# Choosing the FFN units of an agent-attention MoE kernel by two searched limits instead of by a rank over all keys

## The chip, the cores and the metric

The kernel runs on one core of one Trainium2 chip. The metric is device time of the whole launch in microseconds (us), the median of three runs.

## The reference

There are four batches of N = 11456 tokens with 128 channels, and 49 agents per batch. Attention goes from agents to keys and back from queries to agents; its output is the input x of a mixture of eight experts with F = 1024 hidden units, of which each token uses the best one.

```
a2k = softmax(agents @ k.T / sqrt(128));  agent_v = a2k @ v
x   = softmax(q @ agents.T / sqrt(128)) @ agent_v
expert = argmax(normalize(x) @ normalize(expert_emb).T / tau)
out = gate * (relu(x @ w1[expert]) @ w2[expert])
```

So x of a token is a positive mixture of the 49 rows of agent_v, and what it gives at a hidden unit is the same mixture of the 49 values of agent_v @ w1 at that unit.

## The kernel before

For each batch the kernel forms agent_v (`av_chain`), takes the expert that most tokens of the batch will use, loads its w1 and w2 (`load_expert`) and multiplies agent_v by w1 (`gp`, kept in `gts`): 49 values g for each of the 1024 units. A unit whose 49 values have one sign is linear for every token: relu does nothing or gives zero. So the units are sorted by the key (sum g)^2 / (sum g^2), which is 49 where all values are equal and small where signs are mixed:

- the 256 units with the smallest keys (FM = 2 x 128) go through a real relu: their weights are gathered into `gh` and `gl` (high and low halves in 16 bits) and `w2p`;
- all others are taken as linear, and of these the positive ones are summed into one matrix `lin`;
- the next 320 units (FV) are gathered into `vm`, and `proved` tests for every token that their sign is the expected one; the rest is covered by a bound (`far`) on the token's weights. Tokens that fail (strays) are found in `mark_strays` and computed singly by `fix`, or by a loop at the very end.

All of this is `pick_expert`, a generator that is run beside the rest. A unit sits at (partition p, column c) with c from 0 to 7. The rank of a unit was found so: the key is cut to its upper bits and the unit number is written into the lower ones, so that no two are equal (L773 to L777); matmuls with the identity copy all 1024 keys to every partition (`row`, L796, evicted by ScalarE at L798); four passes on VectorE count the smaller keys for columns 0 to 3 (L810) and four on ScalarE sum signs for columns 4 to 7 (L812, corrected at L819). From the rank come one-hot matrices `sel` (L822 for the 256, L899 for the 320), and matmuls with these gather: `placed` (L831) the weights agent_v @ w1, `w2pp` (L871) the rows of w2. L852 makes `lin`.

The whole program is unrolled; a planner sets the order of the instructions on each engine, and every engine then works through its own queue in that order. In batch 0 nothing else is to be done while units are chosen, so there `in_place` fixes an instruction's place behind a named one, and zero matmuls (`zero_products`, ZV, ZG, ZB of them) fill TensorE's queue. In batches 1 to 3 the choice runs beside the FFN of the batch before: `ffn_mm1` (L1222, L1223), evictions `hh` on ScalarE (L1226) and `hl` on VectorE (L1227), `ffn_mm2` (L1250 to L1252), `proved` (L1093 to L1099), and the keys and queries of other batches (L418 to L436). A `yield g` lets the other generators place their work before the next lines.

Of the kernel before, what the change touches and what calls it, by code (L numbers as in the profile page):

```python
# [18 lines left out]
P = 128  # L19
# [10 lines left out]
def kernel(ctx: ExitStack, tc: tile.TileContext, q, k, v, agents, emb, tau, w1, w2, out):  # L30
# [9 lines left out]
    FW = 4 * P  # L40
# [28 lines left out]
    ZV, ZG, ZB = 3, 2, 6  # L69
# [235 lines left out]
    uid = cst.tile([P, NF], I32, name="uid")  # L305
# [22 lines left out]
    def setup():  # L328
# [8 lines left out]
        with in_place(i_):  # L337
            pool.iota(iotaf, pattern=[[1, FW]], base=0, channel_multiplier=0, allow_small_or_imprecise_dtypes=True)
            pool.iota(uid, pattern=[[P, NF]], base=0, channel_multiplier=1)
            pool.iota(iota8m, pattern=[[1, E]], base=64, channel_multiplier=0, allow_small_or_imprecise_dtypes=True)  # L340
            pool.iota(pidx, pattern=[[0, 1]], base=0, channel_multiplier=1, allow_small_or_imprecise_dtypes=True)
        dve.tensor_tensor(out=fold, in0=ident[:, :A], in1=ident[:, LO : LO + A], op=ALU.add)
        with in_place(i_):
# [6 lines left out]
            pool.memset(cnt_p, 0.0)  # L350

    def setup2():

        dve.tensor_scalar(tri, iotaf[:, :P], pidx, None, ALU.is_gt)
# [27 lines left out]
    a_last, f_last, n_last, c_last, v_last = [], [], [], [], []  # L382
# [291 lines left out]
    def pick_expert(b, g):  # L674
# [36 lines left out]
        flat = sel.rearrange("p c f -> p (c f)").bitcast(F32)  # L711
        row = flat[:, F:]
        junk = [sel.rearrange("p c f -> p (c f)")[:, i * F : (i + 1) * F] for i in range(2)]
# [8 lines left out]
        act.activation(junk[0], w1s, AF.Square, accum_out=sq[0])  # L722
# [21 lines left out]
        def second():  # L744
# [14 lines left out]
        mean, key, nkey, sgn, pw = col("mean"), col("key"), col("nkey"), col("sgn"), col("pw")  # L759
        gsq = flat[:, : NF * A].rearrange("p (c a) -> p c a", a=A)  # L760
# [3 lines left out]
        ki = key.bitcast(I32)  # L764
# [43 lines left out]
        rank, more = col("rank"), col("more")  # L808
# [27 lines left out]
        dve.scalar_tensor_tensor(out=mask, in0=rank, scalar=FM - 0.5, in1=pos, op0=ALU.is_ge, op1=ALU.mult)  # L836
# [5 lines left out]
        for h in (1, 0):  # L842
            e_last = vec.tensor_tensor(out=gts[:, :, h, :A], in0=ga, in1=mask.unsqueeze(2).broadcast_to([P, NF, A]), op=ALU.mult)
# [884 lines left out]
```

## Time and profile before

| | |
|---|---|
| median of 3 runs | 704.52 us (702.52 to 705.45) |
| the profiled execution | 704.34 us |
| its span in the profile | 702.5 us |
| TensorE (PE) busy | 646.8 us, 92% of the span |
| VectorE (DVE) busy | 542.2 us, 77% |
| ScalarE (ACT) busy | 488.0 us, 69% |
| GpSimd (POOL) busy | 341.7 us, 49% |

The span is the time from the first to the last instruction of the core; the rest of the device time lies around it. Busy is the sum of an engine's instruction times, and matmuls overlap each other. Times in the timelines count from the span's start. Batch 0 chooses its units between 67 and 87 us, batches 1 to 3 around 217 to 259, 385 to 430 and 545 to 595 us.

### The profile page before, as it was taken

To read this page: it belongs to the slowest core of one execution; us is meant where nothing else is said; L and a number is where in the kernel's file an instruction comes from. 1 tells how busy PE (TensorE), PEld (TensorE's weight loads), DVE (VectorE), ACT (ScalarE), POOL (GpSimd) and SP (SyncE) were. 2 spreads that over 40 slices of the span, in tenths; PEclk is the share of its full clock that TensorE was granted. 3 is DMA by queue.
4 is the path that set the end of the run, shared out by engine and by line. 5 is a ranking of instruction groups with operands and counts; after the bars stand their busy time and mean duration, and the time that the engine had idled before them with its cause. 6 is when DMAs were issued, how large, how long until landed. Compare 5 with 4: busy or idle time off the path is not lost. (4 is left out here: it accounts for less than half of the span.)

```text
span 702.5 us, 23300 instructions
## 1 busy us (share of the span) xinstructions
PE 646.8 (92%) x9168; PEld 531.3 (76%) x9168; DVE 542.2 (77%) x1485; ACT 488.0 (69%) x1350; POOL 341.7 (49%) x578
## 2 busy tenths in 40 slices
PE   8998897999999899899999789899999979998995
PEld 6886786777788587688887568688888768786685
DVE  4755996875669998756777999896576898977993
ACT  3555687797778856687778856868668863878841
POOL 6000247384415836656524553567463563976400
PEclk9998999999999899999999999999999999999999
DMA  8986099959778359949796539949576526233121
GB/s 342 291 277 250 2 242 256 215 154 264 177 238 246 87 141 260 215 149 230 242 239 168 119 84 243 243 127 249 138 182 201 134 74 151 62 92 110 61 79 70
DMA packets 163136, 124.73 MB, mean 178 GB/s; under 512 B 82874, under 2 KB 139280, under 8 KB 163026
## 3 DMA queue, kind: packets, MB, share of 16 engines
q1 hardware_dynamic: 149586, 99.54, 55.3%
q10 hardware_dynamic: 13120, 23.47, 9.8%
q8 instruction: 73, 1.20, 0.7%
q14 instruction: 37, 0.30, 0.1%
q0 software_dynamic: 320, 0.23, 0.1%
HBM read 80.26 MB, written 23.79 MB: 148 GB/s over the span
## 5 line engine op out<-in xcount | busy, mean ns | idle before, releaser
L1227 DVE SCALAR_TENSOR_TENSOR hl<-hp,hh 128x512 f16<-128x512 f32 (+1 forms) x184 | 122.5, 668 | 33.0 <-ACT hh L1226 32.4
L1250 PE MATMUL yp<-w2p,hh 128*128 128x128 f16 x720 | 139.2, 221 | 3.9 <-ACT hh L1226 3.9
L1251 PE MATMUL yp<-w2p,hh 128*128 128x128 f16 x720 | 139.0, 220 | 0.0
L1252 PE MATMUL yp<-w2p,hl 128*128 128x128 f16 x720 | 136.1, 221 | 0.3 <-DVE hl L1227 0.3
L1097 ACT ACTIVATE under<-vp 128x320 f16<-128x320 f32 (+1 forms) x268 | 118.5, 442 | 24.8 <-PE vp L1093 20.1
L1226 ACT ACTIVATE hh<-hp 128x512 f16<-128x512 f32 (+1 forms) x184 | 107.4, 590 | 39.6 <-PE hp L1223 28.3
L1093 PE MATMUL vp<-vm,tt 128*128 128x320 f16 x360 | 96.6, 302 | 7.6 <-ACT under L1097 3.0
L425 ACT COPY fT<-fTp 128x512 f32<-128x512 f32 (+1 forms) x136 | 75.5, 573 | 29.1 <-PE fTp L418 20.6
L436 PEld LDWEIGHTS sp<-aT_all,fT 128*64 128x64 f32 x2336 | 79.9, 138 | 17.9 <-issue 8.4
L436 PE MATMUL sp<-aT_all,fT 128*64 128x49 f32 x2336 | 92.5, 225 | 1.0 <-DVE aT_all L206 0.4
L1250 PEld LDWEIGHTS <-hh 128*128 128x128 f16 x720 | 72.0, 100 | 20.0 <-ACT hh L1226 7.4
L1252 PEld LDWEIGHTS <-hl 128*128 128x128 f16 x720 | 71.5, 99 | 15.4 <-issue 4.7
L1251 PEld LDWEIGHTS <-hh 128*128 128x128 f16 x720 | 71.6, 100 | 5.8 <-issue 0.6
L960 POOL TENSOR_TENSOR e<-qe,e 128x392 f16<-128x392 f32 (+1 forms) x46 | 42.7, 927 | 64.5 <-ACT e L959 62.5
L1222 PE MATMUL hp<-tt,gh 128*128 128x512 f16 (+1 forms) x184 | 69.2, 377 | 4.6 <-DVE vmin L1099 3.6
L1265 DVE TENSOR_TENSOR ot<-yp,gs 128x512 f32<-128x512 f32 (+1 forms) x92 | 61.4, 670 | 11.0 <-PE yp L1252 8.7
L1223 PE MATMUL hp<-tt,gl 128*128 128x512 f16 (+1 forms) x184 | 69.3, 377 | 0.0
L1044 POOL TENSOR_TENSOR nrm<-qq,half 128x16 f32<-128x16 f32 (+2 forms) x28 | 68.9, 2461 | 0.2
L1241 PE MATMUL yp<-lin,tt 128*128 128x128 f16 x720 | 62.0, 220 | 1.2 <-DVE ot L1265 1.2
L1005 POOL TENSOR_TENSOR rt<-rt 128x384 f32<-128x384 f32 (+1 forms) x48 | 40.3, 840 | 43.9 <-DVE rt L1002 42.2
L418 PE MATMUL fTp<-ident,qt 128*128 128x128 f32 (+1 forms) x344 | 55.0, 288 | 5.3 <-ACT under L1097 2.2
L1099 DVE TENSOR_REDUCE vmin<-vp 128x1 f32<-128x320 f32 (+1 forms) x92 | 44.1, 480 | 17.2 <-PE vp L1093 16.8
(359 smaller groups left out, 1575.5 us busy)
## 6 DMA issues: line engine op xcount, KB each, us to landing
kt<-in_k_dram SPq DMA_DIRECT2D x44, 512.0 KB, 7.4
vt<-in_v_dram SPq DMA_DIRECT2D x44, 512.0 KB, 6.5
out_dram<-ot ACTq DMA_DIRECT2D x88, 256.0 KB, 3.1
qt<-in_q_dram SPq DMA_DIRECT2D x42, 512.0 KB, 6.1
w1s<-in_moe_w_dram SPq DMA_DIRECT2D x9, 512.0 KB, 4.3
w2s<-in_moe_w_dram SPq DMA_DIRECT2D x9, 512.0 KB, 6.7
q<-in_q_dram SPq DMA_DIRECT2D x2, 512.0 KB, 11.3
tt<-e SPq DMA_TRANSPOSE x46, 3.9
```

What stands on the lines that cost most here:

```text
L425: act.copy(dst, tp[:, : m * p])
L436: i = pe.matmul(out=s[h : h + w, c * A : (c + 1) * A], lhsT=xT[:, c * p + h : c * p + h + w], rhs=rhs, start=True, stop=True, skip_group_c ...
L1044: pool.tensor_tensor(out=nrm, in0=quad, in1=half[:, :n], op=ALU.pow)
L1093: pe.matmul(out=z[:p, :FV], lhsT=tts[b, u][:, c * p : (c + 1) * p], rhs=bt.vm, start=True, stop=True)
L1097: act.activation(under[:p], z[:p, :FV], AF.Relu, scale=-1.0, accum_out=bt.vsum[:p, at])
L1222: pe.matmul(out=hp[:, :m], lhsT=bt.gh[:, fs], rhs=tt, start=True, stop=False)
L1223: pe.matmul(out=hp[:, :m], lhsT=bt.gl[:, fs], rhs=tt, start=False, stop=True)
L1226: h_last[:] = [act.activation(hh[:, :m], hp[:, :m], AF.Relu)]
L1227: dve.scalar_tensor_tensor(out=hl[:, :m], in0=hp[:, :m], scalar=0.0, in1=hh[:, :m], op0=ALU.max, op1=ALU.subtract)
L1250: pe.matmul(out=y, lhsT=hh[:, cs], rhs=wh, start=False, stop=False, skip_group_check=True)
L1251: pe.matmul(out=y, lhsT=hh[:, cs], rhs=wl, start=False, stop=False, skip_group_check=True)
L1252: y_last[:] = [pe.matmul(out=y, lhsT=hl[:, cs], rhs=wh, start=False, stop=last, skip_group_check=True)]
```

## The change

The rank is replaced by two limits. The key is scaled so that it lies between 0 and 4096. First VectorE compares each of a partition's 8 keys with 64 limits 0, 1, 4, ..., 63^2, and eight matmuls of a column of ones with the result add up over units: every partition gets, for each limit, how many of the 1024 keys are below it. The number of limits with at most 256 (and at most 576) keys below gives the step in which the limit lies. The same is done again with 32 finer limits for each of the two (the wanted counts come in as one more matmul), and the largest finer limit with no more than the wanted count is taken. A unit is a member of the 256, or of the 320, if its key is below its limit; its place is the number of members before it, from matmuls with a triangle (same column) and with ones (columns before). Places that stay empty in the 320 are masked in `vm` by adding 1024 to the test value. The bound `far` comes from the second limit.

In batch 0 the low half of w2 (`w2x[:, :, 1]`) moves from before the rank to after the one-hot writes, the scores of the next batch's units 2 and 3 move behind the first count and behind the placing, and the zero matmuls are divided differently (ZB from 6 to 1, and 2, 4 and 3 before the new groups). The constants `iotaf` start at 1 instead of 0, and `sel` and `vm` get 320 columns instead of 512.

```diff
+    T1, T2 = 64, 32
+    KQ = T1 * T1 / A
...
-    ZV, ZG, ZB = 3, 2, 6
+    ZV, ZG, ZB, ZC = 3, 2, 1, (2, 4, 3)
+    HOP = 2
...
-                act.activation(w2x[:, :, 0], w2s, AF.Copy, scale=s3)
-                with in_place(n_last):
-                    dve.scalar_tensor_tensor(out=w2x[:, :, 1], in0=w2s, scalar=s3, in1=w2x[:, :, 0], op0=ALU.mult, op1=ALU.subtract)
+                s_last[:] = [act.activation(w2x[:, :, 0], w2s, AF.Copy, scale=s3)]
...
-        dve.tensor_tensor(out=key, in0=key, in1=pw, op=ALU.mult)
-        yield 1
-        dve.tensor_scalar(ki, ki, 0x7FFFFC00, None, ALU.bitwise_and)
-        yield 1
-        dve.tensor_scalar(key, key, 2.0 ** -100, None, ALU.max)
-        yield 1
-        dve.tensor_tensor(out=ki, in0=ki, in1=uid, op=ALU.bitwise_or)
-        yield 1
-        n_ = dve.tensor_scalar(nkey, key, -1.0, None, ALU.mult)
...
+        dve.scalar_tensor_tensor(out=key, in0=key, scalar=KQ, in1=pw, op0=ALU.mult, op1=ALU.mult)
+        yield 1
+        def count(i, thrs):
+            n_ = dve.tensor_tensor(out=below[i], in0=key.unsqueeze(2).broadcast_to([P, NF, T1]),
+                                   in1=thrs.unsqueeze(1).broadcast_to([P, NF, T1]), op=ALU.is_lt)
+            if b == 0:
+                n_last[:] = [n_]
+            yield HOP * g
+            t_ = psx("count")
+            if b == 0:
+                zero_products(t_, ZC[i], z_last if i else c_last)
+            t_ = t_[:, :T1]
+            for c in range(NF):
+                i_ = pe.matmul(out=t_, lhsT=one16.broadcast_to([P, P]), rhs=below[i][:, c], start=(c == 0), stop=(c == NF - 1 and i == 0))
+            if i:
+                i_ = pe.matmul(out=t_, lhsT=one16.broadcast_to([P, P]), rhs=caps.rearrange("p k t -> p (k t)"), start=False, stop=True)
+            if b == 0:
+                g_last[:] = [i_]
+                if i == 0:
+                    z_last[:] = ahead_s(2, g_last, pss)
+            yield g
+            return t_
+        t_ = yield from count(0, firsts)
...
+        at, top2 = sm.tile([P, 2], F32, name="at", tag="at"), sm.tile([P, 2], F32, name="top2", tag="top2")
+        for k_, cap in enumerate((FM, FM + FV)):
+            dve.tensor_scalar(below[1][:, k_], t_, cap + 0.5, 0.0, ALU.is_lt, ALU.add, accum_out=at[:, k_ : k_ + 1])
+        yield 1
+        fine = sm.tile([P, 2, T2], F32, name="fine", tag="fine")
+        dve.tensor_tensor(out=fine, in0=steps, in1=at.unsqueeze(2).broadcast_to([P, 2, T2]), op=ALU.add)
+        yield 1
+        dve.tensor_tensor(out=fine, in0=fine, in1=fine, op=ALU.mult)
+        yield 1
+        s3, i3 = yield from second()
+        fine_ = fine.rearrange("p k t -> p (k t)")
+        t_ = yield from count(1, fine_)
...
-        s3, i3 = yield from second()
+        dve.scalar_tensor_tensor(out=fine_, in0=t_, scalar=0.5, in1=fine_, op0=ALU.is_lt, op1=ALU.mult)
+        yield 1
+        dve.tensor_reduce(out=top2, in_=fine, axis=AX.X, op=ALU.max)
+        yield 1
+        dve.tensor_scalar(member[:, 0, :NF], key, top2[:, :1], None, ALU.is_lt)
+        yield 1
+        dve.scalar_tensor_tensor(out=member[:, 1, :NF], in0=key, scalar=top2[:, 1:], in1=member[:, 0, :NF], op0=ALU.is_lt, op1=ALU.subtract)
+        yield HOP * g
+        t_ = psx("place")
+        if b == 0:
+            zero_products(t_, ZC[2], g_last)
+        t_ = t_[:, : 2 * (NF + 1)]
+        pv = t_.rearrange("p (k c) -> p k c", k=2)
+        for c in range(NF + 1):
+            i = pe.matmul(out=pv[:, :, c:], lhsT=one16.broadcast_to([P, P]) if c else tri, rhs=member[:, :, : NF + 1 - c],
+                          start=(c == 0), stop=(c == NF), skip_group_check=True)
+        if b == 0:
+            l_last[:] = [i]
+            z_last[:] = ahead_s(3, l_last, psh)
+            for u in range(2, NEXT):
+                ahead_copy(u, s_last)
...
-        for h in range(2):
-            t_ = psx("row")
-            hs = slice(h * 512, h * 512 + 512)
-            for c in range(NF // 2):
-                i = pe.matmul(out=t_[:, c * P : (c + 1) * P], lhsT=key[:, h * NF // 2 + c : h * NF // 2 + c + 1].broadcast_to([P, P]),
-                          rhs=ident, start=True, stop=True)
-            act.copy(row[:, hs], t_)
-            if b == 0 and h:
-                g_last[:] = [i]
-                z_last[:] = g_last
-                for u in range(2, NEXT):
-                    z_last[:] = ahead_s(u, g_last, psh if u == 3 else pss)
-            yield g
...
-        for c in range(NF // 2):
-            dve.tensor_scalar(junk[0], row, key[:, c : c + 1], 0.0, ALU.is_lt, ALU.add, accum_out=rank[:, c : c + 1])
-            d = c + NF // 2
-            i = act.activation(junk[1], row, AF.Sign, bias=nkey[:, d : d + 1], accum_out=more[:, d : d + 1])
-            if b == 0:
-                s_last[:] = [i]
-            yield g
-        for u in range(2, NEXT) if b == 0 else ():
-            ahead_copy(u, s_last)
-        hi = slice(NF // 2, NF)
-        dve.tensor_scalar(rank[:, hi], more[:, hi], -0.5, (F - 1) / 2, ALU.mult, ALU.add)
+        rank = sm.tile([P, 2, NF], F32, name="rank", tag="rank")
+        dve.scalar_tensor_tensor(out=rank, in0=pv[:, :, :NF], scalar=1.0, in1=member[:, :, :NF], op0=ALU.add, op1=ALU.mult)
+        if b > 0:
+            dve.tensor_scalar(vm, iotaf[:, :FV], pv[:, 1, NF:], 1024.0, ALU.is_gt, ALU.mult)
...
-            dve.tensor_scalar(sel[:, c, :FM], iotaf[:, :FM], rank[:, c : c + 1], None, ALU.is_equal)
+            n_ = dve.tensor_scalar(sel[:, c, :FM], iotaf[:, :FM], rank[:, 0, c : c + 1], None, ALU.is_equal)
...
+        if b == 0:
+            n_last[:] = [n_]
+        if b == 0:
+            with in_place([n_]):
+                dve.tensor_scalar(vm, iotaf[:, :FV], pv[:, 1, NF:], 1024.0, ALU.is_gt, ALU.mult)
+            with in_place(n_last):
+                dve.scalar_tensor_tensor(out=w2x[:, :, 1], in0=w2s, scalar=s3, in1=w2x[:, :, 0], op0=ALU.mult, op1=ALU.subtract)
...
-        dve.scalar_tensor_tensor(out=mask, in0=rank, scalar=FM - 0.5, in1=pos, op0=ALU.is_ge, op1=ALU.mult)
+        dve.scalar_tensor_tensor(out=mask, in0=key, scalar=top2[:, :1], in1=pos, op0=ALU.is_ge, op1=ALU.mult)
...
-            e_last = vec.tensor_tensor(out=gts[:, :, h, :A], in0=ga, in1=mask.unsqueeze(2).broadcast_to([P, NF, A]), op=ALU.mult)
+            with in_place(n_last if b == 0 else ()):
+                e_last = vec.tensor_tensor(out=gts[:, :, h, :A], in0=ga, in1=mask.unsqueeze(2).broadcast_to([P, NF, A]), op=ALU.mult)
...
-        dve.tensor_scalar(mask, rank, FM + FV - 0.5, BIG, ALU.is_lt, ALU.mult)
-        dve.tensor_scalar(rank, rank, -float(FM), None, ALU.add)
-        yield 1
-        dve.tensor_tensor(out=mask, in0=mask, in1=key, op=ALU.add)
-        yield 1
-        dve.tensor_reduce(out=gmx[:, 1:], in_=mask, axis=AX.X, op=ALU.min)
...
+        dve.tensor_scalar(bt.far, top2[:, 1:], -1.0 / KQ, A + 0.1, ALU.mult, ALU.add)
...
-                dve.tensor_scalar(sel[:, c, :FV], iotaf[:, :FV], rank[:, c : c + 1], sgn[:, c : c + 1], ALU.is_equal, ALU.mult)
+                dve.tensor_scalar(sel[:, c, :FV], iotaf[:, :FV], rank[:, 1, c : c + 1], sgn[:, c : c + 1], ALU.is_equal, ALU.mult)
...
-        dve.tensor_scalar(vm, placed(0, FV), thr, None, ALU.subtract)
+        dve.scalar_tensor_tensor(out=vm, in0=placed(0, FV), scalar=thr, in1=vm, op0=ALU.subtract, op1=ALU.add)
```

## Rows read from the trace of the kernel before

**Rows 1.** Timeline of VectorE, batch 0: start us, length us, line, operation.

```profile
69.28 0.17 DVE L771 TENSOR_TENSOR key<-key,pw 128x8 f32<-128x8 f32 x1
...
70.37 0.17 DVE L777 TENSOR_TENSOR key<-key,uid 128x8 int32<-128x8 int32 x1
...
72.13 1.27 DVE L751 SCALAR_TENSOR_TENSOR w1s<-w2s,hsc,w1s 128x1024 f16<-128x1024 f32 x1
...
73.36 1.28 DVE L810 TENSOR_SCALAR_CACHE_REDUCE sel<-sel,key 128x1024 f16<-128x1024 f32 x1
...
77.33 1.28 DVE L810 TENSOR_SCALAR_CACHE_REDUCE sel<-sel,key 128x1024 f16<-128x1024 f32 x1
...
78.61 1.66 DVE L822 TENSOR_SCALAR sel<-iotaf,rank 128x256 f16<-128x256 f16 x8
...
82.54 0.41 DVE L839 CAST gl<-placed 128x256 f16<-128x256 f32 x1
```

**Rows 2.** Timeline of TensorE, batch 0; in brackets idle time and its releaser.

```profile
70.69 2.02 PE L796 MATMUL row<-ident,key 128*128 128x128 f32 x16 [1.47 <-DVE hiv L255]
...
72.64 2.07 PE L436 MATMUL sp<-aT_all,fT 128*64 128x49 f32 x64
...
74.64 1.47 PE L190 MATMUL placed<-zeros 128*128 128x512 f16 x6
...
82.88 1.92 PE L871 MATMUL w2pp<-w1s,sel 128*128 128x256 f16 x16
...
86.97 0.38 PE L1222 MATMUL hp<-tt,gh 128*128 128x512 f16 x1
```

**Rows 3.** Windows: length, busy us (x instructions) PE, PEld, DVE, ACT, POOL; PEclk, DMA, GB/s.

```profile
225.00:245.00 20.00, 16.65 (x155) 11.54 (x154) 18.92 (x52) 17.27 (x47) 16.70 (x28) 0.83 0.44 121
390.00:410.00 20.00, 14.71 (x180) 11.77 (x181) 19.17 (x49) 16.44 (x39) 13.27 (x22) 1.00 0.46 89
560.00:580.00 20.00, 16.15 (x177) 12.86 (x176) 20.00 (x51) 13.07 (x35) 11.44 (x18) 0.91 0.28 77
285.00:390.00 105.00, 99.34 (x1435) 81.52 (x1433) 72.01 (x179) 81.16 (x232) 52.89 (x80) 0.98 0.80 215
```

**Rows 4.** Groups by line, whole run: busy us, mean ns, idle before.

```profile
L810 DVE TENSOR_SCALAR_CACHE_REDUCE sel<-sel,key 128x1024 f16<-128x1024 f32 x16 | 20.4, 1273 | 2.0 <-ACT sel L798 1.9
...
L812 ACT ACTIVATE sel<-sel,nkey 128x1024 f16<-128x1024 f32 x16 | 18.7, 1168 | 0.2
...
L796 PE MATMUL row<-ident,key 128*128 128x128 f32 x64 | 8.5, 281 | 2.6 <-DVE hiv L255 2.6
```

**Rows 5.** Groups by line, nearest to the added comparisons and counts.

```profile
L1161 DVE TENSOR_TENSOR mput<-iotaf,had 128x384 f32<-128x384 f16 x4 | 2.2, 552 | 0.1
...
L1203 DVE TENSOR_SCALAR_CACHE_REDUCE ne<-gid 128x90 f32<-128x90 f32 x32 | 7.6, 239 | 0.3
...
L1203 DVE DVE_READ_ACCUMULATOR ne<-gid 128x1 f32 x32 | 2.6, 82 | 0.0
```

**Rows 6.** Timeline of VectorE, dependent operations on one column.

```profile
62.16 0.16 DVE L251 TENSOR_SCALAR hsc<-total 128x1 int32<-128x1 int32 x1 [0.38 <-PE total L261]
...
62.36 0.15 DVE L253 TENSOR_SCALAR hsc<-hsc 128x1 int32<-128x1 int32 x1
```

**Rows 7.** Timeline of TensorE, first and last of 32 matmuls of 58 columns.

```profile
75.95 0.19 PE L982 MATMUL rtp<-r_hi,tt 128*128 128x58 f16 x1
...
76.78 0.19 PE L983 MATMUL rtp<-r_lo,tt 128*128 128x58 f16 x1
```

**Rows 8.** Timeline of GpSimd, batch 2's selection.

```profile
390.24 1.89 POOL L753 TENSOR_TENSOR w2s<-w2s,hsc 128x1024 f32<-128x1024 f32 x1 [1.37 <-DVE hsc L253]
...
395.44 2.13 POOL L756 TENSOR_TENSOR w1s<-w2s,w1s 128x1024 f16<-128x1024 f32 x1
```

**Rows 9.** Timeline of VectorE in the same stretch.

```profile
390.68 1.48 DVE L779 TENSOR_SCALAR nkey<-key 128x8 f32<-128x8 f32 x1
...
395.74 1.28 DVE L810 TENSOR_SCALAR_CACHE_REDUCE sel<-sel,key 128x1024 f16<-128x1024 f32 x1 [0.55 <-ACT sel L798]
```

More of the change, by code (lines that the diff above doesn't have):

```diff
@@ L39 @@
     FVS = [P * 5 // 2] * B
-    FW = 4 * P
+    FW = max(FVS)
+    T1, T2 = 64, 32
+    KQ = T1 * T1 / A
     TICKS = 4
@@ L304 @@
     tri = cst.tile([P, P], F16, name="tri")
-    uid = cst.tile([P, NF], I32, name="uid")
+    steps = cst.tile([P, 2, T2], F32, name="steps")
+    firsts = cst.tile([P, T1], F32, name="firsts")
+    caps = cst.tile([P, 2, T2], F16, name="caps")
+    one16 = cst.tile([P, 1], F16, name="one16")
+    member = cst.tile([P, 2, NF + 1], F16, name="member")
     def sqrt_into(dst, x, p, n, tag):
@@ L350, in setup @@
             pool.memset(cnt_p, 0.0)
+            pool.iota(firsts, pattern=[[1, T1]], base=0, channel_multiplier=0, allow_small_or_imprecise_dtypes=True)
+            pool.iota(steps, pattern=[[0, 2], [1, T2]], base=0, channel_multiplier=0, allow_small_or_imprecise_dtypes=True)
+            pool.tensor_tensor(out=firsts, in0=firsts, in1=firsts, op=ALU.mult)
+            pool.tensor_scalar(steps, steps, 1.0 / T2, -1.0, ALU.mult, ALU.add)
+            pool.memset(caps[:, 0], -float(NMS[0] * P) / P)
+            pool.memset(caps[:, 1], -float(NMS[0] * P + FVS[0]) / P)
+            pool.memset(one16, 1.0)
+            pool.memset(member, 0.0)
     def setup2():
-        dve.tensor_scalar(tri, iotaf[:, :P], pidx, None, ALU.is_gt)
+        dve.tensor_scalar(tri, iotaf[:, :P], pidx, 1.0, ALU.subtract, ALU.is_gt)
         emb_sq = cst.tile([E, D], F32, name="emb_sq")
@@ L381 @@
     z_last, q_last = [], []
[L382 removed]
+    a_last, f_last, n_last, c_last, v_last, l_last = [], [], [], [], [], []
     k_last, m_last, d_last, r_last, s_last, g_last = [], [], [], [], [], []
@@ L710, in pick_expert @@
         sq = [sm.tile([P, 1], F32, name="wsq%d" % i, tag="wsq%d" % i) for i in range(2)]
-        flat = sel.rearrange("p c f -> p (c f)").bitcast(F32)
-        row = flat[:, F:]
-        junk = [sel.rearrange("p c f -> p (c f)")[:, i * F : (i + 1) * F] for i in range(2)]
+        flat = sel.rearrange("p c f -> p (c f)")
+        junk = flat[:, :F]
+        below = [flat[:, F + i * NF * T1 : F + (i + 1) * NF * T1].rearrange("p (c t) -> p c t", t=T1) for i in range(2)]
         ga = gts[:, :, 0, :A]
@@ L720, in col @@
             return sm.tile([P, NF], dt, name=nm, tag=nm)
-        act.activation(junk[0], w1s, AF.Square, accum_out=sq[0])
+        act.activation(junk, w1s, AF.Square, accum_out=sq[0])
         gp = psx("gp")
@@ L757, in second @@
             return s3, i3
-        mean, key, nkey, sgn, pw = col("mean"), col("key"), col("nkey"), col("sgn"), col("pw")
-        gsq = flat[:, : NF * A].rearrange("p (c a) -> p c a", a=A)
+        mean, key, sgn, pw = col("mean"), col("key"), col("sgn"), col("pw")
+        gsq = flat.bitcast(F32)[:, : NF * A].rearrange("p (c a) -> p c a", a=A)
         act.activation(gsq, ga, AF.Square)
@@ L763, in pick_expert @@
         yield 1
-        ki = key.bitcast(I32)
         dve.tensor_reduce(out=pw, in_=gsq, axis=AX.X, op=ALU.add)
@@ L783, in pick_expert @@
+        t_ = yield from count(0, firsts)
         i = act.copy(gs_[0], gg)
         if b == 0:
-            n_last[:], h_last[:] = [n_], [i]
+            h_last[:] = [i]
+        gmx, pos = sm.tile([P, 1], F32, name="gmx", tag="gmx"), col("pos")
+        with in_place(n_last if b == 0 else ()):
+            dve.tensor_scalar(sgn, mean, 0.0, -0.5, ALU.is_ge, ALU.add)
+            dve.tensor_scalar(pos, mean, 0.0, None, ALU.is_ge)
+            dve.tensor_reduce(out=gmx, in_=ga, axis=AX.XY, op=ALU.max, apply_absolute_value=True)
@@ L806, in pick_expert @@
+        for c in range(NF + 1):
[6 more added lines that the diff above has]
+                ahead_copy(u, s_last)
+        yield g
         if b > 0:
             pool.tensor_tensor(out=gs_[1], in0=gg, in1=gs_[0], op=ALU.subtract)
-        rank, more = col("rank"), col("more")
@@ L842, in pick_expert @@
         for h in (1, 0):
-            e_last = vec.tensor_tensor(out=gts[:, :, h, :A], in0=ga, in1=mask.unsqueeze(2).broadcast_to([P, NF, A]), op=ALU.mult)
+            with in_place(n_last if b == 0 else ()):
+                e_last = vec.tensor_tensor(out=gts[:, :, h, :A], in0=ga, in1=mask.unsqueeze(2).broadcast_to([P, NF, A]), op=ALU.mult)
         if b == 0:
@@ L883, in pick_expert @@
         bt.iall = iall
-        dve.tensor_scalar(mask, rank, FM + FV - 0.5, BIG, ALU.is_lt, ALU.mult)
-        dve.tensor_scalar(rank, rank, -float(FM), None, ALU.add)
         yield 1
-        dve.tensor_tensor(out=mask, in0=mask, in1=key, op=ALU.add)
-        yield 1
-        dve.tensor_reduce(out=gmx[:, 1:], in_=mask, axis=AX.X, op=ALU.min)
-        yield 1
-        dve.tensor_scalar(gmx[:, 1:], gmx[:, 1:], -1.0, None, ALU.mult)
-        top = yield from allmax(gmx, 2, "gmxr", psx, 1)
+        top = yield from allmax(gmx, 1, "gmxr", psx, 1)
         thr = sm.tile([P, 1], F32, name="thr", tag="thr")
         bt.far = sm.tile([P, 1], F32, name="far", tag="far")
-        dve.tensor_scalar(thr, top[:, :1], 2.0 ** -11 + 2.0 ** -16, 2.0 ** -23, ALU.mult, ALU.max)
-        dve.tensor_scalar(bt.far, top[:, 1:], A + 0.1, None, ALU.add)
+        dve.tensor_scalar(thr, top, 2.0 ** -11 + 2.0 ** -16, 2.0 ** -23, ALU.mult, ALU.max)
+        dve.tensor_scalar(bt.far, top2[:, 1:], -1.0 / KQ, A + 0.1, ALU.mult, ALU.add)
         for c in range(NF):
             with in_place([bt.o_] if b == 0 else ()):
-                dve.tensor_scalar(sel[:, c, :FV], iotaf[:, :FV], rank[:, c : c + 1], sgn[:, c : c + 1], ALU.is_equal, ALU.mult)
+                dve.tensor_scalar(sel[:, c, :FV], iotaf[:, :FV], rank[:, 1, c : c + 1], sgn[:, c : c + 1], ALU.is_equal, ALU.mult)
             if c % 4 == 3:
                 yield g
-        dve.tensor_scalar(vm, placed(0, FV), thr, None, ALU.subtract)
+        dve.scalar_tensor_tensor(out=vm, in0=placed(0, FV), scalar=thr, in1=vm, op0=ALU.subtract, op1=ALU.add)
         bt.vm = vm
@@ L978, in q_unit @@
         s = (pss if ffn_at[0] else psh)("rtp")
-        with in_place(g_last if early else y_last):
+        with in_place((l_last if u else g_last) if early else y_last):
             for c in range(n):
@@ L1187, in mark_strays @@
         last = sm.tile([P, 1], F32, name="had2", tag="had2", bufs=1)
-        dve.tensor_scalar(last, had[:, :1], P - KEEP + 0.5, BIG, ALU.is_gt, ALU.mult)
+        dve.tensor_scalar(last, had[:, :1], P - KEEP + 1.5, BIG, ALU.is_gt, ALU.mult)
         yield 1
```

9 lines of the change are left out of this document (2 added, 7 removed).

## The prediction

> **What bounds the kernel now.** I read four views in this order: the busy time by windows, the timeline of VectorE and of TensorE through the first batch's selection, the groups by line, and the timelines of GpSimd and VectorE side by side in a later selection.
>
> Two different things bound the kernel at the places which the change touches. In batch 0 the selection is a bare chain: until the gathered weights exist, no FFN matmul can start. The key is finished at 69.28 + 0.17 = 69.45 us, but then it is packed with the unit number (until 70.37 + 0.17 = 70.54), copied across the partitions and compared. The four rank passes run from 73.36 with a step of (77.33 - 73.36) / 3 = 1.32 us, the first one-hot write starts at 78.61 [rows 1], and the first FFN product at 86.97 [rows 2]. So 9.16 us lie between key and one-hot writes, and nothing of the FFN is there to hide them.
>
> In batches 1 to 3 the selection lies beside the FFN of the batch before. In the three windows that hold it, VectorE is busy 18.92, 19.17 and 20.00 of 20 us, and TensorE runs 155, 180 and 177 matmuls; the stretch of 105 us between two selections has VectorE at 72.01 us and TensorE at 1435 matmuls, which is 273 in 20 us [rows 3]. There VectorE is what the end of the window waits for: its FFN evictions stand in one queue with the rank passes of 1.27 us [rows 4]. Elsewhere TensorE is the fuller engine, so a microsecond of TensorE idleness saved in a selection window comes off the end.
>
> **Batch 0, step by step.** Removed are the packing, the row products (eight, two passes each, 2.02 us [rows 2]), two row copies, and four rounds of one pass on VectorE and one on ScalarE. In their place stand:
> - first comparison, 512 columns. The nearest row is a broadcast comparison of 384 columns at 0.55 us [rows 5]; scaled by columns alone that would be 0.73, with a fixed part less, and I take 0.68;
> - VectorE to TensorE: from the key's last write at 70.54 to the row matmul at 70.69 are 0.15 us [rows 1, 2]. Eight matmuls of 64 columns: 32 of 58 columns start within 76.78 - 75.95 = 0.83 us, 0.027 each, and one lasts 0.19 [rows 7]; so 0.19 + 7 x 0.027 = 0.38. Together 0.53;
> - two counts of 64 columns with an accumulator read: 0.24 + 0.08 each at 90 columns [rows 5], 0.64;
> - two small operations that need each other: 0.20 from start to start [rows 6], 0.40;
> - second comparison 0.68, then 0.15 + 0.19 + 8 x 0.027 = 0.56 for nine matmuls;
> - four small dependent operations 0.80, nine placing matmuls 0.56, the rank 0.20.
>
> This makes 5.05 us. It can't all be bare: the maximum, the signs and the low half of the weights stand behind the comparisons on VectorE, and on TensorE the scores of the next batch's unit 2 (half of 64 matmuls in 2.07 us [rows 2], 1.03) and 2, 4 and 3 zero matmuls of about 0.25 (six in 1.47 [rows 2]) stand between the groups. The scores and four zero matmuls need about 2.0 us against 0.64 + 0.40 + 0.68 + 0.15 = 1.87 of VectorE work, so they just fit. I add 1.2 us for such misfits, an estimate, and get 6.25. Against 9.16 that is a gain of **2.9 us**. The ends: all bare, 9.16 - 5.05 = 4.1; and nothing, if the planner puts as much before the groups as ScalarE and VectorE are freed of.
>
> From the one-hot writes to the first FFN product nothing shortens. What moves there is the low half of the second weights: 1.27 us of VectorE at 72.13, which today ends just as the rows arrive at 73.36 [rows 1], for nothing. Now it follows the one-hot writes, with the new mask (about 0.26, from 1.66 / 8 = 0.21 for a one-hot write of 256 columns [rows 1], for 320). It is needed by the product that starts 82.88 - 78.61 = 4.27 us after the first one-hot write [rows 2], and 1.66 + 0.26 + 1.27 = 3.19 us of VectorE come first [rows 1]. So the placing products hide it, with 1 us to spare; without that cover it would cost up to 1.27. The cast to the low weights at 82.54 [rows 1] comes later by as much, and the FFN, behind two more products, does not see it. No DMA belongs to the moved steps; the transposes and loads that SP issues afterwards hang on the queries' own chain and move along. The new constants on GpSimd are written in the first tens of us and read after 69; they cost nothing.
>
> **Batches 1 to 3.** VectorE loses 4 x 1.32 = 5.3 us each, and gains two comparisons and two counts, 2 x 0.68 + 2 x 0.32 = 2.0. Ten small operations go (packing, negation, correction of the rank, limit and minimum) and eight small ones come; I set them against each other. Net 3.3 us of VectorE a batch. ScalarE loses four passes of 1.17 [rows 4] and two copies. TensorE loses 2.0 us of row products and gets 26 small matmuls, 26 x 0.027 = 0.7: net 1.3. How much of VectorE's 3.3 reaches the end no row shows: nothing, if the planner's other work (marking the strays, evictions) takes the place; all of it and TensorE's 1.3, 4.6 us, if VectorE alone held TensorE. The windows with VectorE at 95 to 100% stand nearer to the upper end, but the marking of strays is in the same windows and stays; I take half of VectorE's, 1.65 a batch, **5.0 us** for three. TensorE's granted clock is 0.83 and 0.91 in two of the windows [rows 3]; what shorter waits may give back of it is not priced.
>
> A place where the change could pay for itself: in a later selection an 8-column VectorE operation takes 1.48 us from 390.68 while a GpSimd product runs from 390.24 to 392.13 [rows 8, 9]. A rank pass that starts at 395.74 inside GpSimd's product of 395.44 to 397.57 keeps its 1.28 us [rows 8, 9]. So the passes that go are of a kind that is not held up, and some that come may be. The Trainium skill (SBUF — State Buffer, "SBUF: two separate sides") says that a VectorE operation with two inputs in SBUF and a GpSimd operation that reads SBUF exclude each other for the whole of an instruction; these two pairs of rows agree with it. By that rule both comparisons are of the held kind, and it is a rival below; the removed packing and minimum operations were exposed in the same way, so by the rows I change nothing.
>
> **Sum.** The profiled execution took 704.34 us (span 702.5), next to the median of 704.52. 704.34 - 2.9 - 5.0 = **696.4 us**. What a measurement here can tell from no change is about 0.5%, 3.5 us: 701.0 to 708.0 is "same".
>
> **Rivals.**
> - Only batch 0 gains. For it: TensorE is busy nearly throughout in the long stretch of [rows 3], and the planner may only move its work. Against: VectorE's 20.00 of 20. Time 704.34 - 2.9 = 701.4. Chance 0.14.
> - Everything reaches the end: 4.1 + 3 x 4.6 = 17.9, time 686.4. For it: the matmul counts of the windows, a third to over two fifths under the long stretch's. Against: the strays' marking stays. Chance 0.11.
> - Slower, by TensorE's queue. Each batch now has three groups (two counts and the placing) that TensorE meets in order and that wait for VectorE; before there was one, the row products, and it did wait: 1.47 us in batch 0 [rows 2], 2.6 in all [rows 4]. Behind a waiting group stand the FFN products of the batch before, and ScalarE's and VectorE's evictions wait for those. Nine groups in three batches at 1.47 are 13.2 us, and with the gain of 7.9 the time is 709.6. It decides from 7.9 / 9 = 0.88 us of wait a group. Against it: two yields are put between each comparison and its products, so that other work can stand between. Chance 0.10.
> - GpSimd holds the comparisons up. Six of them in batches 1 to 3, against GpSimd products of 1.89 and 2.13 us [rows 8]: 3 x 4.02 = 12.1 at most, half of it 6.0 if they meet at random; 704.34 - 2.9 - 5.0 + 6.0 = 702.4. Against it: the removed small operations stood under the same products. Chance 0.07.
> - The change doesn't do what it says: limits on a grid could choose fewer units, so that more tokens stay unproved and the loop at the end runs. Worked out from the reference's inputs, the grid gives 256 and 320 units in three batches and 256 and 319 in the last, and the same 74, 48, 21 and 66 tokens to look at as ranks do. Chance 0.01; a pass of that loop is priced by no row, and I put it over 704.
>
> **How the numbers follow.** The forecast has 0.57, with its own range of 690 to 701. Faster by over 0.5%: nearly all of it, the case in which all arrives, and a fraction of the batch-0 case, 0.73. Same: most of the batch-0 case and GpSimd's, 0.16. Slower: the queue's case and the loop, 0.11. The range of 688 to 704 leaves out the slower cases and half of the best one.
>
> **What would show it.** Batch 0: the first one-hot write about 6 us after the key instead of 9, and the first FFN product near 84.1. If the product comes no earlier although the one-hot writes do, the moved low half or the new mask holds it. Batches 1 to 3: VectorE below 18 of 20 us in the selection's windows and more matmuls in them; TensorE's waits before the count products under 0.9 us; comparisons near 0.68 us, and over 1.5 us if GpSimd holds them. The prediction is wrong if the windows' matmul counts stay as they were, if TensorE waits over 0.88 us for each group, or if the first FFN product does not move.

## The result, and the profile after

The changed kernel takes 709.89 us (median of 6 runs, 707.99 to 715.03), the kernel before 702.87 on the same chips (6 runs, 700.44 to 705.45). The ratio is 1.0119, 95% interval 1.0086 to 1.0152: slower by 7.0 us between the medians and by 8.4 by the ratio, where a time of 696.4 was forecast. The ratio is worked out over all runs and is not the quotient of the two medians. The profiled execution took 708.08 us, its span is 706.3.

**Batch 0's chain got shorter, as forecast, up to the one-hot writes.** VectorE after (start us, length us, line, operation), in the stretch that answers to [rows 1]:

```profile
66.31 0.20 DVE L780 RECIPROCAL pw<-pw 128x8 f32<-128x8 f32 x1
66.55 0.17 DVE L782 SCALAR_TENSOR_TENSOR key<-key,pw 128x8 f32<-128x8 f32 x1
66.81 0.69 DVE L787 TENSOR_TENSOR sel<-key,firsts 128x512 f16<-128x512 f32 x1
...
69.70 0.68 DVE L787 TENSOR_TENSOR sel<-key,fine 128x512 f16<-128x512 f32 x1
...
72.92 1.66 DVE L861 TENSOR_SCALAR sel<-iotaf,rank 128x256 f16<-128x256 f16 x8
...
74.71 1.28 DVE L870 SCALAR_TENSOR_TENSOR w1s<-w2s,hsc,w1s 128x1024 f16<-128x1024 f32 x1
...
77.47 0.41 DVE L885 CAST gl<-placed 128x256 f16<-128x256 f32 x1
```

From the finished key (66.55 + 0.17 = 66.72) to the one-hot writes it is 6.20 us; 6.25 was forecast, 9.16 stood there. But the first FFN product, TensorE's hp, gained far less. TensorE after, against [rows 2]:

```profile
76.51 1.07 PE L432 MATMUL fTp<-ident,qt 128*128 128x128 f32 x8
77.41 1.91 PE L918 MATMUL w2pp<-w1s,sel 128*128 128x256 f16 x16
79.25 0.55 PE L450 MATMUL sp<-aT_all,fT 128*64 128x49 f32 x10
79.73 2.05 PE L899 MATMUL linp<-w2s,gts 128*128 128x128 f32 x16
81.72 0.90 PE L450 MATMUL sp<-aT_all,fT 128*64 128x49 f32 x22
...
83.15 0.38 PE L1262 MATMUL hp<-tt,gh 128*128 128x512 f16 x1
```

One-hot to product is 83.15 - 72.92 = 10.23 us, 8.36 before [rows 1, 2]. The 10 + 22 score matmuls of query unit 2 (0.55 + 0.90 us) now stand between w2pp and hp. So 1.09 of the 2.96 us gained are left there.

The product itself stands 3.82 us earlier (86.97 to 83.15), but 2.73 of that are no gain of the change: in this execution the reciprocal, the last operation that both kernels have, is that much earlier (69.05 to 66.31). Over all the profiled executions shown here it lies between 66.3 and 70.0 us, with ranks and with limits alike.

**Then the head start turns into a delay.** SyncE's own queue, before (first fence) and after (second); each line is one DMA issue or several (x) in a row, its length is how long the queue stood at them:

```profile
87.71 1.36 SPq L971 DMA_TRANSPOSE tt<-e  x1
89.17 1.48 SPq L157 DMA_DIRECT2D kt<-in_k_dram  x3
...
119.48 8.51 SPq L539 DMA_TRANSPOSE kT<-ks  x2
```

```profile
91.57 1.36 SPq L1011 DMA_TRANSPOSE tt<-e  x1
93.03 1.48 SPq L160 DMA_DIRECT2D kt<-in_k_dram  x3
94.61 6.57 SPq L553 DMA_TRANSPOSE kT<-ks  x1
...
127.25 10.37 SPq L553 DMA_TRANSPOSE kT<-ks  x2
```

In both kernels the next batch's key loads (kt) stand in this queue behind the first query transpose, which waits for query unit 2. That transpose is 3.86 us later though the FFN starts 3.82 earlier; counted from the reciprocal, it is 6.60 later and the FFN 1.08 earlier. Windows 132 to 148 us, of before, of after (length, busy us (x instructions) of PE, PEld, DVE, ACT, POOL, then TensorE's granted clock, DMA share, GB/s), and TensorE's longest wait between 100 and 146 us in both (us in total, times, longest):

```profile
132.00:148.00 16.00, 15.71 (x240) 12.79 (x237) 12.69 (x28) 13.84 (x44) 9.08 (x16) 1.00 0.47 134
...
PE sp L548 <- DMA kT<-ks: 2.7, 1, 2.7
```

```profile
132.00:148.00 16.00, 9.81 (x133) 7.86 (x135) 5.78 (x11) 6.59 (x23) 0.25 (x2) 0.68 0.79 160
...
PE sp L562 <- DMA kT<-ks: 6.8, 1, 6.8
```

TensorE waits 6.8 us for a transposed key until 138.06, and behind the idle time its granted clock falls: between 138 and 142 us it is 0.50, the lower of its two levels (1.2 and 2.4 GHz), and its mean over the window is 0.68. Counting the FFN's products with `gh` from 0 in both traces, product 12 starts 6.0 us earlier than before (130.35 against 136.38), product 14 starts 2.6 later (144.91 against 142.31): 8.6 us are lost there.

**Batches 1 to 3.** The windows of [rows 3], after:

```profile
225.00:245.00 20.00, 14.62 (x181) 9.90 (x181) 19.73 (x58) 14.29 (x41) 15.48 (x23) 0.86 0.41 108
390.00:410.00 20.00, 15.39 (x219) 11.94 (x217) 19.86 (x61) 12.36 (x36) 14.13 (x23) 0.92 0.54 127
560.00:580.00 20.00, 16.87 (x216) 14.37 (x215) 19.38 (x50) 9.88 (x27) 14.20 (x21) 0.83 0.34 98
```

There are 26 to 39 more matmuls in each, but VectorE is as full as it was. Batch 3's selection became longer, not shorter (VectorE before in the first fence, after in the second):

```profile
550.25 0.19 DVE L769 RECIPROCAL pw<-pw 128x8 f32<-128x8 f32 x1
...
569.50 1.01 DVE L822 TENSOR_SCALAR sel<-iotaf,rank 128x256 f16<-128x256 f16 x1
...
578.43 0.37 DVE L839 CAST gl<-placed 128x256 f16<-128x256 f32 x1
```

```profile
550.93 0.18 DVE L780 RECIPROCAL pw<-pw 128x8 f32<-128x8 f32 x1
...
553.80 0.63 DVE L787 TENSOR_TENSOR sel<-key,firsts 128x512 f16<-128x512 f32 x1
...
557.04 0.21 DVE L818 TENSOR_SCALAR_CACHE_REDUCE sel<-count 128x64 f16<-128x64 f32 x1
...
564.48 1.99 DVE L882 SCALAR_TENSOR_TENSOR mask<-key,top,pos 128x8 f32<-128x8 f32 x1
566.62 0.82 DVE L837 SCALAR_TENSOR_TENSOR member<-key,top,member 128x8 f16<-128x8 f32 x1
...
574.18 0.10 DVE L856 SCALAR_TENSOR_TENSOR rank<-place,member 128x16 f32<-128x16 f32 x1
...
576.29 1.65 DVE L861 TENSOR_SCALAR sel<-iotaf,rank 128x256 f16<-128x256 f16 x8
...
580.35 0.41 DVE L885 CAST gl<-placed 128x256 f16<-128x256 f32 x1
```

Two of these operations are long beside their work (1.99 and 0.82 us; see the last section), the others cost little; between them the queue does the FFN's evictions and the strays. From the reciprocal to the one-hot writes it is, in batches 1, 2 and 3, 14.1, 18.4 and 19.3 us before, and 12.8, 14.3 and 25.4 after. To the cast of `gl`, the low weights, it is 24.3, 26.1 and 28.2 us before, and 19.9, 24.3 and 29.4 after: the first selection gained 4.5 us, the last lost 1.2. The last two products of batch 2 start at 571.42 and 576.82 before and at 566.45 and 574.05 after, the first of batch 3 at 577.86 and 579.59: a lead of 5.0 us becomes a lag of 1.7. With ranks the high weights `gh` were there at 575.33, 2.5 us ahead of batch 3's first product; with limits they are there at 578.67, and batch 3's FFN waits for the selection.

### The profile page after: what moved, and what is told of

Its sections match the earlier page's. It is cut to its first block, busy times and chain, and to the rows that moved or that the text cites. A ratio compares the mean times of both kernels' runs of the same rounds, so it can differ in the third digit from the quotient of the medians.

```text
span 706.3 us, 23332 instructions
## 1 busy us (share of the span) xinstructions
PE 644.7 (91%) x9212; PEld 529.2 (75%) x9212; DVE 537.0 (76%) x1469; ACT 466.8 (66%) x1310; POOL 343.8 (49%) x585
## 5 line engine op out<-in xcount | busy, mean ns | idle before, releaser
L1292 PEld LDWEIGHTS <-hl 128*128 128x128 f16 x720 | 71.9, 100 | 14.3 <-issue 3.2
L1305 DVE TENSOR_TENSOR ot<-yp,gs 128x512 f32<-128x512 f32 (+1 forms) x92 | 61.6, 671 | 12.2 <-PE yp L1292 7.9
L1084 POOL TENSOR_TENSOR nrm<-qq,half 128x16 f32<-128x16 f32 (+2 forms) x28 | 70.4, 2515 | 0.2
L1137 ACT ACTIVATION_READ_ACCUMULATOR under<-vp 128x1 f32 (+1 forms) x268 | 55.0, 205 | 0.0
```

The lines of the kernel that those rows point to most:

```text
L1084: pool.tensor_tensor(out=nrm, in0=quad, in1=half[:, :n], op=ALU.pow)
L1137: act.activation(under[:p], z[:p, :FV], AF.Relu, scale=-1.0, accum_out=bt.vsum[:p, at])
L1292: y_last[:] = [pe.matmul(out=y, lhsT=hl[:, cs], rhs=wh, start=False, stop=last, skip_group_check=True)]
```

## The experiments

Theory A: batch 0's new order makes the key loads late. Theory B: the later selections cost more than they save. All ratios are to the kernel before, run beside each on one chip. Each is good to some 0.2 to 0.6%, so a difference of two of them, given below in us of 703, is good to some 3 us, and to 4 where x1_first is one of the two.

### Which batches lose

```
-    pick_expert: the new selection in all batches
+    pick_expert = new selection if b in NEW else ranks      # NEW = (), (0,), (1, 2, 3)
```

The edit is shortened; where batch 0 has ranks, its zero matmuls are also divided as before (ZB is 6).

> Control: the rank method in all four batches, in the frame of the changed kernel (its constants, iota from 1, so that the narrow one-hot writes subtract 1 before they compare). Theory A (the changed order around batch 0 makes the loads restart late) and theory B (three round trips between VectorE and TensorE in each later selection) both expect the time of the kernel before, 702.9 us within 0.5%: 699.4 to 706.4. Theory C (any rewrite that shuffles the planner's order moves the time by a per cent) expects a time outside that.

Measured: 0.9993 (0.9955 to 1.0030). The frame costs nothing.

> The new selection in batch 0 alone, ranks in batches 1 to 3. Theory A: the first FFN product at 83 us as in the changed kernel, the loads restart behind 91 us, TensorE waits 5 us or more for a transposed key near 131 to 138 us, and the time is 705 to 709 us. Theory B: batch 0 keeps its gain of about 3 us and the time is 699 to 701.

Measured: 1.0184 (1.0127 to 1.0241), 715.73 us, more than the whole change. The first product is at 83.45 us, the loads restart at 93.33, TensorE waits 7.9 us for the transposed key. Theory A's signs are all there, its size was too low.

> Ranks in batch 0, the new selection in batches 1 to 3. Theory A: the later selections together give back 0 to 4 us, 699 to 703. Theory B: nine round trips cost more than they save and the time is 707 to 712. Both expect the first FFN product near 87 us.

Measured: 1.0019 (0.9990 to 1.0047). That lies between both ranges: the later selections give and take the same. In its trace the FFN of batch 2 runs 9.4 us ahead of x0_none at product 136 (batch 2's last tile), and is level again (0.1 us) by product 160. Of the 9.4 us, 6.5 go between products 136 and 138, where the FFN of batch 3 begins: batch 3's chain to `gl` takes 28.0 us here and 28.6 in x0_none, so what the FFN beside it won is lost where batch 3 needs the weights.

### Is it the loads?

```
-            with in_place(w_last if b == 0 or now[0] // 2 < start + 2 else t_last):
+            with in_place(w_last if b == 0 or now[0] // 2 < start + 10 else t_last):
```

> The changed kernel with three more key loads and one query load put ahead of the first query transpose in SyncE's queue. Theory A: the loads restart before 80 us instead of at 93, the wait of 6.8 us for the transposed key near 131 us shrinks below 3, and the time falls by 4 to 7 us, to 703 to 706. Theory B: under 2 us change, 708 to 711.

Measured: 1.0032 (0.9998 to 1.0067), 705.30 us, about 6 us less than the changed kernel by the ratios (4.6 between the medians, from two chips). The three loads are issued between 65.20 and 80.32 us. In the window 132 to 148 TensorE is busy 15.88 us again. Its waits for transposed keys did not shrink below 3 us as expected: there are two, 7.0 us in all.

> Control for e1_after_10: the kernel before with its next three key loads put ahead of the first query transpose in SyncE's queue; the order on the other four engines is the same. Theory A: the kernel before loses little to the late restart (its wait for the transposed key is 2.7 us), so it gains 0 to 3 us, 701 to 704. Rival: the edit is good for 5 us in any kernel and has nothing to do with the change; then about 698 to 699.

Measured: 1.0008 (0.9974 to 1.0041). The edit gains nothing for the kernel before: it mends what the change broke. One reservation on the traces: in the profiled executions of both kernels of this edit, TensorE's granted clock is 0.72 between 60 and 72 us (0.94 before, 1.00 after), and from the reciprocal to the first product it is 21.53 us (17.92 before) and 18.17 (16.84 after). The five later runs with early loads, 15.38 to 16.84, do not show this; why these two do is open.

> x1_first (the new selection in batch 0 alone) with the early loads of e1_after_10. If the late loads are all of batch 0's loss: 702 to 705, at or a little below the kernel before. If they are the 6 us that e1_after_10 measured and the rest of x1_first's 12 is the planner's order in batch 2's selection: 708 to 711.

Measured: 1.0005 (0.9979 to 1.0032), against x1_first's 1.0184. The first case: with the loads early, all of batch 0's loss is gone. Not all of it was lost at the keys: x1_first is 3.5 us behind e13_x1_loads at product 14, 6.5 at 46 and 8.6 at 104. How the rest hangs on the loads, and why batch 0 alone loses twice what the whole change loses by them, is not shown. Window, waits and SyncE's queue of e13_x1_loads:

```profile
132.00:148.00 16.00, 15.88 (x206) 12.92 (x205) 9.41 (x20) 11.96 (x41) 5.30 (x9) 0.90 0.30 90
...
PE sp L565 <- DMA kT<-ks: 6.7, 2, 4.2
...
59.81 19.09 SPq L161 DMA_DIRECT2D kt<-in_k_dram  x4
...
92.52 1.36 SPq L1249 DMA_TRANSPOSE tt<-e  x1
...
118.16 11.18 SPq L556 DMA_TRANSPOSE kT<-ks  x2
```

The pair of key transposes is back near 119 us (127.25 in the changed kernel). But TensorE still waits 6.7 us for keys, and between products 10 and 12 the 4.7 us by which this kernel was ahead of before are gone (0.2 behind). Against x0_none, whose reciprocal stands within 0.2 us of this one's, 5.8 us of lead shrink to 1.0 at the same place: an FFN that starts earlier only waits longer for the keys. With its loads mended, the new selection in batch 0 is worth nothing that 0.3% can tell.

### Why is the query transpose late?

From the reciprocal to that transpose it is 18.66 us before and 25.26 after. Before, unit 2's maximum (qmx) stood ahead of the 8 wide one-hot writes on VectorE; the chain of the minimum, which the change removed, came before these and probably kept them back (not tested by itself). ScalarE then took the unit at once: its two steps on it start 0.57 us apart, at 84.72 and 85.29. After, the writes are first, and ScalarE meets the unit amid the keys' casts, with 1.94 us between the two steps. VectorE before (first fence), VectorE after (second) and ScalarE after (third):

```profile
83.51 0.55 DVE L948 TENSOR_REDUCE qmx<-sp 128x8 f32<-128x392 f32 x1
...
86.56 1.22 DVE L899 TENSOR_SCALAR sel<-iotaf,rank,sgn 128x320 f16<-128x320 f16 x2
```

```profile
80.76 2.84 DVE L939 TENSOR_SCALAR sel<-iotaf,rank,sgn 128x320 f16<-128x320 f16 x8
...
84.74 0.55 DVE L988 TENSOR_REDUCE qmx<-sp 128x8 f32<-128x392 f32 x1
...
86.55 0.54 DVE L991 TENSOR_TENSOR qe<-sp,qmx 128x392 f32<-128x392 f32 x1
```

```profile
87.83 0.58 ACT L994 ACTIVATE qe<-qe 128x392 f32<-128x392 f32 x1
88.27 1.19 ACT L542 ACTIVATE ks<-kt,hsc 128x1024 f16<-128x1024 f32 x1
...
89.77 0.58 ACT L999 CAST e<-qe 128x392 f16<-128x392 f32 x1
```

Two edits of the changed kernel, both shortened:

```
-            z_last[:] = ahead_s(3, l_last, psh)          # behind the placing
+                    z_last[:] = ahead_s(3, z_last, psh)  # behind the first count   (e2_unit3)
...
-            with in_place([bt.o_] if b == 0 else ()):
+            with in_place(e_last if b == 0 else ()):     # unit 2's qe              (e8_wide_after_q2)
```

> The changed kernel with the scores of the next batch's key unit 3 moved back from behind the placing to behind the first count, together with unit 2. Theory A in its first form (the moved unit makes the lead query units late): query unit 2's transposes come earlier, the first query DMA transpose goes before 89.5 us instead of at 91.6, and the time falls to 703 to 706. Rival: query unit 2 is late because the 8 wide one-hot writes of 2.84 us and the first FFN evictions stand before its maximum on VectorE; then the transpose stays at 91 us or later and the time at 708 to 711.

Measured: 1.0057 (1.0030 to 1.0085). Reciprocal to transpose 22.78 us, to the first product 16.31 (16.84 in the changed kernel). The transpose, at 90.32, and the time, 706.78, lie between both expectations; the interval ends just below the changed kernel's.

> The changed kernel with batch 0's 8 wide one-hot writes (320 columns) put behind query unit 2's maximum and subtraction on VectorE, as they stood before the change. Theory A: the first query DMA transpose goes at 87 to 89 us instead of 91.6, the loads restart with it, and the time falls to 703 to 706. Rival (ScalarE, fuller in this stretch, holds the unit anyway): transpose at 90 or later, 707 to 711.

Measured: 1.0070 (1.0040 to 1.0099), 709.83 us. Time and transpose both lie in the rival's ranges. But its head ran 2.7 us later in the profiled execution, so the transpose stands at 91.59; from the reciprocal it is 22.57 us, 2.7 earlier than in the changed kernel. Its interval overlaps that kernel's, so a gain in time is not shown, only the earlier transpose. Each edit mends 2.5 to 2.7 of the 6.6 us; that the two add and that the rest is ScalarE's was not tested.

### Batch 3

Both edits stand on e1_after_10, with its early loads.

```
-    HOP = 2
+    HOP = 0                                              # e3_hop0
...
-            spawn(pick_expert(b, 1), 1, half=True)
+            spawn(urgent(pick_expert(b, 1), 2) if b == B - 1 else pick_expert(b, 1), 1, half=True)
```

> e1_after_10 with no steps put between a comparison and its products in batches 1 to 3 (HOP 0 for 2). Theory B2 (the steps between stretch the last selection, and the FFN of batch 3 waits for it): from batch 3's key to its first one-hot write about 18 us instead of 24, and 701 to 704 us. Rival (the steps hide TensorE's waits, as the forecast had it): TensorE waits 0.9 us or more for each of nine groups and the time is 707 to 712.

Measured: 1.0022 (0.9989 to 1.0056), not to be told from e1_after_10's 1.0032. Reciprocal to one-hot of batch 3 fell from 24.4 to 15.4 us, further than expected, and between products 128 and 176 the FFN won 4.5 us on e1_after_10; but between 96 and 104, in batch 2's selection, it had lost 4.4. Why stays open.

> e1_after_10 with batch 3's selection issued two steps at a time at high priority, as batch 0's is. Theory B2: batch 3's first FFN product comes 3 to 6 us earlier against the end of batch 2's, and the time is 700 to 703 us. Rival (the FFN of batch 2 pays for what goes ahead of it): 705 to 707, no change from e1_after_10.

Measured: 0.9913 (0.9885 to 0.9941), 697.93 us: faster than both kernels. Batch 3 in e6_urgent3 on VectorE, and the GpSimd product beside its second comparison:

```profile
544.12 0.20 DVE L780 RECIPROCAL pw<-pw 128x8 f32<-128x8 f32 x1
...
549.83 2.29 DVE L787 TENSOR_TENSOR sel<-key,fine 128x512 f16<-128x512 f32 x1
...
558.50 1.79 DVE L861 TENSOR_SCALAR sel<-iotaf,rank 128x256 f16<-128x256 f16 x8
...
564.56 0.40 DVE L885 CAST gl<-placed 128x256 f16<-128x256 f32 x1
...
549.68 1.89 POOL L765 TENSOR_TENSOR w2s<-w2s,hsc 128x1024 f32<-128x1024 f32 x1 [4.96 <-DVE hsc L256]
```

Reciprocal to one-hot is 14.38 us, and 20.44 to gl (29.42 in the changed kernel).

> Control for e6_urgent3: the kernel before with batch 3's selection (ranks) issued two steps at a time at high priority. If e6's gain of 7 us comes from what the change saves in batches 1 to 3 being let through, the kernel before gains less, 0 to 3 us: 700 to 703. Rival: the priority alone is worth it, whichever selection stands there: 694 to 698.

Measured: 1.0051 (1.0023 to 1.0079), slower. With ranks the same priority makes batch 3 as short (14.46 and 20.54 us), and the kernel slower; so e6's gain is not the priority's alone. In the kernel before `gh` had 2.5 us to spare, so no FFN was waiting for that chain. The windows 545 to 565 us of e7_before_u3 and of e6_urgent3 say where it differs:

```profile
545.00:565.00 20.00, 15.79 (x183) 12.50 (x182) 18.54 (x45) 15.41 (x42) 6.65 (x11) 1.00 0.17 51
```

```profile
545.00:565.00 20.00, 18.87 (x267) 15.86 (x267) 17.86 (x56) 13.51 (x36) 10.10 (x14) 1.00 0.28 83
```

With ranks TensorE does 183 matmuls beside the selection, with limits 267: VectorE and ScalarE have as much to do, but with ranks four passes on each (5.1 and 4.7 us) stand in place of FFN evictions (6 on VectorE and 5 on ScalarE, with limits 8 and 7).

> The changed kernel with that priority in batch 3 and nothing else, SyncE's queue as it was. If the loss of batch 0 and that of batch 3 are separate and add: 709.9 less 7 is 702 to 704, with TensorE still waiting 6 us or more for the transposed key near 131 us. Rival: the gain needs the early loads: 707 or more.

Measured: 0.9998 (0.9972 to 1.0024), about 8.5 us less than the changed kernel; TensorE's wait for the key is 4.7 us here, not 6. In its trace the FFN wins 7.0 us on the changed kernel between products 128 and 138, where batch 3 begins. With e1_after_10's 6.1 the 8.5 make 14.6, and e6_urgent3 is 14.5 below: within some 3 us the two losses are separate and add.

> x2_later (ranks in batch 0, the new selection in batches 1 to 3) with the priority in batch 3, SyncE's queue as it was. If batch 3's loss of about 8 us is its own and batch 0's order has no part in it: 705 less 6 to 8, 696 to 699, the level of e6_urgent3, and the new selection in batch 0 is then worth nothing by itself. Rival (the gain of e6 needs batch 0's shorter chain): 701 or more.

Measured: 0.9924 (0.9898 to 0.9950), 697.93 us, the level of e6_urgent3 with ranks in batch 0. The later selections are then worth 5.3 us (0.76% of 703.14).

> e6_urgent3 with the priority in batches 1 and 2 as well. If a later selection's length matters only where the next batch's FFN waits for it, batches 1 and 2 have slack and it changes nothing or costs a little: 697 to 701 against 697.9. If every selection holds the FFN up: 692 to 695.

Measured: 0.9982 (0.9955 to 1.0009), 703.94 us: 0.7% worse than e6_urgent3 and worse than either expectation, though the selections got shorter (to 12.1, 12.2 and 12.5 us). In batches 1 and 2 no FFN waits for the chain: in e6_urgent3 `gl` is there at 240.7 and 409.1, and the first products of those batches stand at 255.9 and 413.9. So its length is no price there; the likely price is the work that is put behind it, for between products 30 and 46, beside batch 1's selection, the FFN of e9_all_urgent falls 6.2 us further behind e6_urgent3's.

> e6_urgent3 with unit 3's scores back behind the first count, as in e2_unit3. If query unit 2's lateness still costs once the loads go ahead of it: 694 to 696.5. If the loads were all that hung on it: 697 to 699, as e6_urgent3.

Measured: 0.9944 (0.9921 to 0.9966), 699.70 us. Nothing is won by an earlier query unit (21.84 us from the reciprocal to its transpose, 25.25 in e6_urgent3) once the loads go ahead of it; the loads were what hung on it.

## Why the prediction was wrong, point by point

- **Key to one-hot, 6.25 us**: right (6.20), and so were the comparison (0.68 forecast, 0.69) and the counts.
- **One-hot to product "unchanged 8.36"**: wrong by 1.87. The moved low half was hidden as argued. What was not seen is that unit 2's scores, which before stood between the placing products (80.48 and 82.28), come behind w2pp when the placing comes earlier.
- **"No DMA belongs to the moved steps; the transposes and loads that SP issues afterwards hang on the queries' own chain and move along."** This is the step that failed in batch 0. They moved 6.6 us the other way. The wide one-hot writes passed unit 2's maximum (2.7 us, e8_wide_after_q2) and unit 3's scores went behind the placing (2.5, e2_unit3); that ScalarE's FFN work came earlier is read from the trace alone. One transpose waits for all of these, and the loads for it. Price: 6.1 us (e1_after_10) of the whole change, 12.6 when batch 0 alone is changed (1.0184 to 1.0005).
- **Batch 0's 2.9 us**: only 1.1 reaches the first product, and none of it the end, even with early loads (e13_x1_loads; and e6_urgent3 and e12_x2_u3, with limits and with ranks in batch 0, take the same 697.93 us), since the keys for the next batch, not the FFN's start, set the pace near 130 us.
- **Batches 1 to 3, 1.65 us each, from VectorE's busy time**: the sum of 5.0 is what e12_x2_u3 shows (5.3), but only with batch 3's selection let through. As built, batch 3's chain to `gl` took 29.4 us where ranks took 28.2, and the FFN, which was 5.0 us ahead, came to wait for it; let through, it takes 20.4 and the kernel 8.5 us less (e7_after_u3). This is the step that failed in the later batches: the prediction priced what the new operations occupy and not how long a chain with two more round trips, and steps put between, takes in a shared queue; where the next FFN waits for the chain, its length is the price. VectorE "below 18 of 20 us" did not come either (19.4 to 19.9).
- **Rival "slower by TensorE's queue", 709.6 us**: the time came true, its mechanism did not. In batches 1 to 3 TensorE waited 0.5, 0.4 and 0.0 us before the counts and 0.6, 0.5 and 1.7 before the placing, 3.7 in nine groups (0.41 each), and the 1.7 was for another operation (rt). The point from which it decides, 0.88, was not reached on the mean. That the time is near 709.6 is chance. TensorE waited elsewhere.
- **Rival "GpSimd holds the comparisons"**: seen in e6_urgent3 (2.29 us, 0.68 free), but not in the changed kernel, whose six later comparisons take 0.63 to 0.85 us. The pair of rows that the prediction put beside the rule of two inputs is of another kind: nkey has one input in SBUF, and it was held to the end of the product all the same (392.16 against 392.13 [rows 8, 9]). The rank pass, which keeps its time, has one input too. Which operations with one input are held the runs do not show.

The forecast of 696.4 is close to e6_urgent3's 697.93 by luck: the sizes differ, nothing from batch 0 and some 5 from the later batches, and that only with two repairs that the forecast did not have.

## What to carry to other kernels

When an early stage is shortened, follow each in-order queue behind it to the next load, and ask what else the removed operations held back: here eight writes passed the one unit on whose transpose all loads hung. A chain that runs beside other work is to be priced by its length from start to end where something waits for it, not by the engine time that it saves. Control a repair on the kernel before: the early loads gained nothing there, so they were a repair and not a find.

## What the runs showed of the hardware

An 8-column operation on VectorE with two inputs in SBUF (mask, from key and pos) took 1.99 us at 564.48 and 0.22 in batch 0, and a 512-column comparison 2.29 us instead of 0.68, each started while GpSimd ran a product of 1024 columns. The first ends, at 566.47, with this product (GpSimd after):

```profile
564.33 2.13 POOL L768 TENSOR_TENSOR w1s<-w2s,w1s 128x1024 f16<-128x1024 f32 x1 [0.71 <-ACT w1s L767]
```

The Trainium skill (SBUF — State Buffer, "SBUF: two separate sides") says that a VectorE operation with two inputs in SBUF and a GpSimd operation that reads SBUF exclude each other for a whole instruction; these rows agree, 8-column operations too.

The DMA transposes of keys got slower: the median from issue to landing of the four between 84 and 150 us is 5.9 us before, 9.5 after and 10.4 in e13_x1_loads. In e13_x1_loads they start as early as before (the pair at 118.16, against 119.48), so starting late is not the reason. What is, was not tested.
